# Sigmoid attention by pairs of heads: scores by halves of TensorE's rows, plain float32 sums for every head

## The chip, the core and the metric

One Trainium2 chip, of which one core is used. The metric is the device time of the program in microseconds. The kernel before takes 1150.06 us (median of three runs, 1149.88 to 1151.21). Its profile is of one execution of 1148.2 us.

The engines go by the profile's names: PE is TensorE's matrix products and PEld its weight loads, DVE is VectorE, ACT is ScalarE, POOL is GpSimd, SP is SyncE, which here only issues DMAs. Each engine works through its own queue in order.

## The reference

Three stages one after the other, for 4 batches of 448 tokens:

```python
scores = q @ k.transpose(0, 1, 3, 2) / sqrt(64) - log(448)   # 4 x 12 heads, 448 x 448
x = sigmoid(scores) @ v                                      # no softmax; heads side by side: 768 columns

h = maximum(x @ w_in, 0); u, v = h[..., :512], h[..., 512:]  # gated unit
v = normalised over its 512 columns
x = (u * (w_spatial @ v + b_spatial)) @ w_out

xn = normalised(x) * g_ln                                    # channel MLP, 768 -> 3072 -> 768
out = x + maximum(xn @ w_ch1, 0) @ w_ch2
```

The weights w_in, w_out, w_ch1 and w_ch2 come as numbers of 8 bytes.

## The kernel before, in words

**Products in parts.** A float32 number is split into a high part in the type float32r and a low part, the difference (`split`: a cast on ACT, a subtraction on DVE or POOL). A product of two such numbers is three products of parts (`mm3`, L246 to L248: high by high, high by low, low by high). A product of plain float32 is one instruction (it shows as two records in the trace) and needs no split, but goes over the data more often.

**Order.** Nothing is scheduled by the compiler: each engine's order is the order in which the Python code lays instructions out. Three mechanisms mix the work. The loop over heads lays out attention. A `Stream` named `bg` yields TensorE work of the gated unit (`hv`: x by the v half of w_in, 512 columns; `hu`: by the u half, 448 columns) in amounts counted in estimated us, `BG_0` and `BG_US` a head, and yields nothing as long as its inputs aren't there (`settled`: laid out `LAG` heads before). `Jobs` hands out pieces of the preparation of w_in and w_out: `load` (a DMA of 768 KB on SP's queue, into one of two raw buffers), `decode` (8 bytes to float32: L264 on ACT, L265, L266 and L269 on DVE) and `split` (L275 on ACT, L276 on DVE). w_in has 8 blocks of 768 columns, w_out 4. Heads from `FIRST` = 3 on hand out one piece each, from `MORE` = 14 on two; w_out's are queued after head `WO_FROM` = 38. After attention the rest of `bg` is laid out at once, then the last batch's `hv` and `hu`, `spatial`, the projection with w_out and the channel MLP.

**Scores** (`qk`, L433). A pair of heads is prepared together. Its tile `kk` holds k's high part in partitions 0 to 63 and k's low part in 64 to 127, and q's high part lies in both halves. For a chunk of 128 keys, one product over all 128 rows gives high by high plus low by high; a second over 64 rows, with k's high and q's low part, gives the third term. A head has four chunks, done in two calls of two: two 128-row products, two 64-row products, then one sigmoid (L438, ACT) over both chunks. High parts come by casting DMAs on POOL's queue (`qk_cast`, L367 and L368), the float32 numbers by SP's (`qk_load`, L377 and L378), and the low parts are subtracted by POOL (`qk_split`, L408 and L409; the first pairs by DVE). The first pair has its own path (`first_pair`).

**Weighted sums** (`av`). For heads 0 to 18 (`PLAIN`) four plain float32 products (L464) with v as weights, 64 columns wide, put in turn into the two column halves of the array, so that the two halves of the output's partitions hold parts of the sum. For the other 29 heads the sigmoids are split (`a_split`: L447 on ACT, L449, L451, L453, L454 on DVE), v is split (`v_split`), and seven products of parts over the full array follow (L470, L472); again each half of the partitions holds parts of the sum. In both cases `a_end` adds the halves (L484 copy on ACT, L485 add on DVE), and after two heads `x_split` splits x for the gated unit (by POOL from batch 2 on).

**Shapes.** TensorE's instructions thus come in three shapes: 128 rows by 128 columns (the high scores products, the split sums, all of the gated unit and MLP), 64 by 128 (the low scores products) and 128 by 64 (plain sums). PSUM has four banks for single tiles (`ps1`) and two tiles of two banks (`ps2`, scores).

Of the kernel before, what the change touches and what calls it, by code (L numbers as in the profile page):

```python
# [16 lines left out]
P = 128  # L17
# [21 lines left out]
# Matrix work of the gated unit beside each head, in us: in the first batch, and after.  # L39
BG_0, BG_US = 2.5, 2.2  # L40
# Heads after which what was laid out counts as there.
LAG = 2
WARM = 10
# The last batches whose low parts of v and x come from the vector engine.
V_POOL, X_POOL = 0, 1
# [10 lines left out]
R_ATT, F_ATT = 15872, 6208  # L56
R_MLP, F_MLP = 11904, 9984
# Where blocks lie after attention: none meets another while both are in use.
# [10 lines left out]
class Arena:  # L69
    """Columns of tiles that are given out and taken back while the program is laid out."""  # L70
# [89 lines left out]
class Jobs:  # L160
    """Pieces of work that are laid out between others, in order."""
# [42 lines left out]
def sigmoid_attention_gmlp_mlp(ctx: ExitStack, tc, q, k, v, w_in, w_sp, w_out, g_ln, w1, w2, out):  # L204
# [54 lines left out]
    def w_decode(raw):  # L259
# [3 lines left out]
        # The scale moves the exponent's offset from 1023 to 127; what float32 has not, goes to zero.  # L263
# [14 lines left out]
    class Chunk:  # L278
        """768 columns of a weight: load, decode and split are laid out apart."""
# [33 lines left out]
    def idle():  # L313
# [13 lines left out]
    # The blocks that stay past attention come first, from the base.  # L327
# [3 lines left out]
    x_r = Ring(F, S, 2)  # L331
    R.add("att", r_att)
    F.add("att", f_att)
    qh_r = Ring(R, 2 * S, 3, "att")
    ql_r = Ring(R, 2 * S, 2, "att")
    kk_r = Ring(R, 2 * SK, 3, "att")
    vv_r = Ring(R, 1024, 2, "att")
    ah_r = Ring(R, 4 * S, 2, "att")
    al_r = Ring(R, 3 * S, 2, "att")
    rv = Ring(F, 512, 3, "att")  # L340
    rq = Ring(F, 2 * S, 1, "att")
    rk = Ring(F, 2 * SK, 1, "att")
    af_r = Ring(F, 2 * S, 2, "att")
    tmp_r = Ring(F, S, 1, "att")
    v0_r = Ring(F, DH, 1, "att")
    a_rings = [v0_r, qh_r, ql_r, kk_r, vv_r, ah_r, al_r, rv, rq, rk, tmp_r]

    heads = [(b, h) for b in range(B) for h in range(H)]
    pairs = {}
    head = {}  # L350
# [6 lines left out]
    def plain(i):  # L357
        return i in PLAIN

    def on_pairs(f):  # L360
        return lambda p: f(p, *divmod(p, NPAIR)) if p < B * NPAIR else None

    @on_pairs
    def qk_cast(p, b, hp):
        """The high parts: q's in both halves of the partitions, k's in the first."""
        qh, kk = qh_r.next().ap(2, S), kk_r.next().ap(2, SK)
        nc.gpsimd.dma_start(kk[:D], k[b, hp])  # L367
        nc.gpsimd.dma_start(qh, q[b, hp])  # L368
        pairs[p] = dict(qh=qh, kk=kk)
# [10 lines left out]
    def first_pair():  # L380
        """The first pair's parts, head by head, without the wait for the casting DMAs."""
        qh, kk, ql = qh_r.next().ap(2, S), kk_r.next().ap(2, SK), ql_r.next().ap(2, S)
        qr, kr = rq.next().ap(2, S), rk.next().ap(2, SK)
        pairs[0] = dict(qh=qh, kk=kk, ql=ql)
        for j in range(2):
            nc.sync.dma_start(kr[:D, j], k[0, 0, :, j])
            nc.sync.dma_start(qr[:, j], q[0, 0, :, j])
        yield
        for j in range(2):
            nc.scalar.copy(kk[:D, j], kr[:D, j])  # L390
            nc.vector.tensor_copy(qh[:, j], qr[:, j])
            nc.vector.tensor_sub(kk[D:P, j], kr[:D, j], kk[:D, j])  # L392
            nc.vector.tensor_sub(ql[:D, j], qr[:D, j], qh[:D, j])
            yield
# [16 lines left out]
    @on_pairs  # L411
    def v_split(p, b, hp):
        t = pairs[p]
        vr = t["v"]
        vv = t["vv"] = vv_r.next().ap(8, 2, D)
        js = [j for j in range(2) if not plain(2 * p + j)]
        if js:
            cs = slice(4 * js[0], 4 * js[-1] + 4)
            split(vv[:, cs, 0, :], vv[:, cs, 1, :], vr[:, cs], nc.gpsimd if b > V_POOL else nc.vector)

    def qk(i, t):
        p, j = divmod(i, 2)
        a = pairs[p]
        if t == 0:
            head[i] = dict(af={})
            if not plain(i):
                head[i].update(ah=ah_r.next().ap(4, S), al=al_r.next().ap(3, S))
        ps = ps2()
        for part in ("qh", "ql"):
            rows = P if part == "qh" else D  # L430
            for cc in range(2):
                kc = slice((2 * t + cc) * P, (2 * t + cc + 1) * P)
                nc.tensor.matmul(  # L433
                    ps[:, cc, :S], a["kk"][:rows, j, kc], a[part][:rows, j],
                    start=(part == "qh"), stop=(part == "ql"),
                )
        af = af_r.next().ap(2, S)
        nc.scalar.activation(af, ps[:, :, :S], AF.Sigmoid, bias=bias_s, scale=1.0 / math.sqrt(D))  # L438
        head[i]["af"][t] = af

    def a_split(i, t, on_act):
        if plain(i):
            return
        h = head[i]
        ah, al, af = h["ah"], h["al"], h["af"].pop(t)
        if on_act:
            nc.scalar.copy(ah[:, 2 * t : 2 * t + 2], af)  # L447
        else:
            nc.vector.tensor_copy(ah[:, 2 * t : 2 * t + 2], af)  # L449
        if t == 0:  # L450
            nc.vector.tensor_sub(al[:, 0:2], af, ah[:, 0:2])  # L451
        else:
            nc.vector.tensor_sub(al[:, 2], af[:, 0], ah[:, 2])  # L453
            nc.vector.tensor_sub(ah[D:P, 3], af[D:P, 1], ah[D:P, 3])  # L454

    def av(i):
        p, j = divmod(i, 2)
        h = head[i]
        ps = ps1()
        for c in range(4):  # L460
            if plain(i):
                # In turn to the two halves of the array's columns, which run beside each other.
                rows = slice(D * (c % 2), D * (c % 2) + D)
                nc.tensor.matmul(  # L464
                    ps[rows, :S], pairs[p]["v"][:, 4 * j + c], h["af"][c // 2][:, c % 2],
                    start=(c < 2), stop=(c > 1),
                )
                continue
            w = pairs[p]["vv"][:, 4 * j + c].rearrange("p a d -> p (a d)")
# [5 lines left out]
    def a_end(i):  # L475
# [3 lines left out]
        if j == 0:  # L479
            pairs[p]["x"] = x_r.next().ap(S)  # L480
# [340 lines left out]
    for _ in pair0:  # L821
        pass
# [221 lines left out]
```

## Time and profile before

| | us |
|---|---|
| median of three runs | 1150.06 |
| profiled execution, first to last instruction | 1148.2 |
| busy: TensorE | 1131.0 |
| busy: VectorE | 727.0 |
| busy: ScalarE | 384.9 |
| busy: GpSimd | 218.2 |
| last scores product begins at | 293.3 |
| granted clock of TensorE, mean over the span | 0.991 of full speed |

A group's row in the profile has the line, engine, operation, what is written and read with shapes, the count, then the busy time in us, the mean length of one in ns, and the engine's idle time just before them with what ended it. A product's end in the trace is modelled, and products run into one another, so the distance between starts tells more than the length. Forms such as 64*128 are the rows and columns of the array that an instruction uses.

### The profile page before, as it was taken

What the parts mean: (1) busy time and instruction counts of PE and PEld (TensorE: products, weight loads), DVE (VectorE), ACT (ScalarE), POOL (GpSimd) and SP (SyncE); (2) the same over time, 40 slices, a digit from 0 to 9 for tenths busy, and PEclk for the clock granted to TensorE, in tenths of its full rate; (3) what the DMA queues carried; (4) which work ended last, traced back from release to release, by engine and by line L of the source; (5) the groups of instructions that cost most, each with busy time, mean ns of one, the idle gap of its engine ahead of it and who ended that gap; (6) DMA issues with size and microseconds to landing.
All of it is one profiled execution on the core that took longest, in us unless ns stands there. A gap on an engine that the chain in (4) does not pass through costs nothing.

```text
span 1148.2 us, 14874 instructions
## 1 busy us (share of the span) xinstructions
PE 1131.0 (99%) x6071; PEld 1019.7 (89%) x6071; DVE 727.0 (63%) x928; ACT 384.9 (34%) x586; POOL 218.2 (19%) x167
## 2 busy tenths in 40 slices
PE   8998999998999999999999999999999999999998
PEld 4445776776899999999999999999999999999998
DVE  3879999989677577545455555555554545555533
ACT  4776666665545243211112121111212112121100
POOL 2765556864221442000000000000000000000000
PEclk8999999998999999999999999999999999999999
DMA  9887444662641111111111111111111112020013
GB/s 251 234 220 196 119 129 122 151 186 86 216 133 65 69 56 56 55 56 55 56 56 56 55 56 55 55 56 56 56 56 55 56 36 76 28 83 28 28 74 120
DMA packets 33557, 104.81 MB, mean 91 GB/s; under 512 B 7568, under 2 KB 10128, under 8 KB 33360
## 3 DMA queue, kind: packets, MB, share of 16 engines
q1 hardware_dynamic: 26736, 79.93, 21.7%
q0 software_dynamic: 6752, 23.92, 8.0%
q8 instruction: 48, 0.79, 0.3%
q14 instruction: 21, 0.17, 0.1%
HBM read 90.98 MB, written 12.86 MB: 90 GB/s over the span
## 4 chain that ended last, share of the span: by engine, by line
PE 85%; DVE 9%; issue 3%; ACT 1%; DMA 0%; SPq 0%; ACTq 0%; DVEq 0%
PE ps L246 26%; PE ps L247 25%; PE ps L248 25%; PE ps L433 5%; DVE r_att L454 2%; DVE r_att L449 1%; PE ps L464 1%; PE ps L470 1%; DVE r_att L453 1%; DVE r_att L451 1%; DVE r_base L276 1%; DVE f_base L485 1%; DVE f_base L265 1%; PE ps L679 1%; PE ps L472 1%
## 5 line engine op out<-in xcount | busy, mean ns | idle before, releaser
L246 PE MATMUL ps<-r_base 128*128 128x384 f32 (+3 forms) x756 | 258.0, 341 | 0.0
L247 PE MATMUL ps<-r_base 128*128 128x384 f32 (+3 forms) x756 | 253.7, 336 | 0.1
L248 PE MATMUL ps<-r_base 128*128 128x384 f32 (+3 forms) x756 | 253.7, 336 | 0.0
L735 DVE TENSOR_TENSOR f_mlp<-ps,f_mlp 128x768 f32<-128x768 f32 (+1 forms) x157 | 149.5, 953 | 160.0 <-PE ps L248 159.9
L716 ACT ACTIVATE r_mlp<-ps 128x384 fp32r<-128x384 f32 (+1 forms) x120 | 56.4, 470 | 513.3 <-PE ps L248 513.3
L717 DVE SCALAR_TENSOR_TENSOR r_mlp<-ps,r_mlp 128x384 fp32r<-128x384 f32 (+1 forms) x120 | 63.5, 529 | 152.0 <-ACT r_mlp L716 152.0
L246 PEld LDWEIGHTS ps<-r_base 128*128 128x128 f32 x756 | 142.6, 189 | 16.7 <-issue 12.7
L248 PE MATMUL ps<-r_mlp 128*128 128x384 f32 (+1 forms) x460 | 154.5, 336 | 0.0
L246 PE MATMUL ps<-r_mlp 128*128 128x384 f32 x448 | 150.6, 336 | 0.0
L247 PE MATMUL ps<-r_mlp 128*128 128x384 f32 x448 | 150.3, 336 | 0.0
L248 PEld LDWEIGHTS ps<-r_base 128*128 128x128 f32 x756 | 142.8, 189 | 5.2
L247 PEld LDWEIGHTS ps<-r_base 128*128 128x128 f32 x756 | 142.8, 189 | 3.9 <-DVE r_base L276 0.4
L433 PE MATMUL ps<-r_att 64*128 64x448 f32 (+1 forms) x384 | 117.7, 408 | 3.6 <-DVE r_att L392 3.6
L433 PEld LDWEIGHTS ps<-r_att 64*128 64x128 f32 (+1 forms) x384 | 63.7, 192 | 54.3 <-issue 39.3
L246 PE MATMUL ps<-r_mlp,r_base 128*128 128x384 f32 (+1 forms) x304 | 105.3, 346 | 0.0
L247 PE MATMUL ps<-r_mlp,r_base 128*128 128x384 f32 (+1 forms) x304 | 104.3, 343 | 0.0
L248 PE MATMUL ps<-r_mlp,r_base 128*128 128x384 f32 (+1 forms) x292 | 99.8, 342 | 0.0
L438 ACT ACTIVATE f_att<-ps,bias_s 128x896 f32<-128x896 f32 x76 | 76.6, 1008 | 65.3 <-PE ps L433 30.2
L248 PEld LDWEIGHTS ps<-r_mlp 128*128 128x128 f32 x460 | 86.4, 188 | 0.2
L246 PEld LDWEIGHTS ps<-r_mlp 128*128 128x128 f32 x448 | 84.2, 188 | 0.0
L247 PEld LDWEIGHTS ps<-r_mlp 128*128 128x128 f32 x448 | 84.1, 188 | 0.0
L247 PE MATMUL ps<-r_base,r_mlp 128*128 128x384 f32 x224 | 76.3, 341 | 0.0
(120 smaller groups left out, 1681.5 us busy)
## 6 DMA issues: line engine op xcount, KB each, us to landing
f_base<-in_w SPq DMA_DIRECT2D x48, 768.0 KB, 4.2
r_att<-in_q POOLq DMA_DIRECT2D x23, 448.0 KB, 4.5
f_att<-in_v SPq DMA_DIRECT2D x24, 256.0 KB, 3.9
f_base<-in_w_in SPq DMA_DIRECT2D x8, 768.0 KB, 5.7
r_att<-in_k POOLq DMA_DIRECT2D x23, 256.0 KB, 4.0
f_att<-in_k SPq DMA_DIRECT2D x22, 256.0 KB, 3.5
f_att<-in_q SPq DMA_DIRECT2D x24, 224.0 KB, 3.5
out_y<-f_mlp SPq DMA_DIRECT2D x12, 384.0 KB, 2.3
```

The lines of the kernel that those rows point to most:

```text
L246: nc.tensor.matmul(ps, lh, rh, start=first, stop=False)
L247: nc.tensor.matmul(ps, lh, rl, start=False, stop=False)
L248: nc.tensor.matmul(ps, ll, rh, start=False, stop=last)
L265: nc.vector.tensor_scalar(bits, bits, 3, None, op0=ALU.logical_shift_left)
L276: eng.tensor_sub(lo, x, hi)
L433: nc.tensor.matmul(ps[:, cc, :S], a["kk"][:rows, j, kc], a[part][:rows, j], start=(part == "qh"), stop=(part == "ql"),)
L438: nc.scalar.activation(af, ps[:, :, :S], AF.Sigmoid, bias=bias_s, scale=1.0 / math.sqrt(D))
L449: nc.vector.tensor_copy(ah[:, 2 * t : 2 * t + 2], af)
L454: nc.vector.tensor_sub(ah[D:P, 3], af[D:P, 1], ah[D:P, 3])
L716: nc.scalar.activation(hh[:, f], ps[:, :n], AF.Relu)
L717: nc.vector.scalar_tensor_tensor(hl[:, f], ps[:, :n], 0.0, hh[:, f], op0=ALU.max, op1=ALU.subtract)
L735: nc.vector.tensor_add(y[:, hs], ps, y[:, hs])
```

## The change

Attention is done by pairs of heads instead of by heads, with one call for half a pair's keys. There are 48 such calls, as there were 48 heads.

- **Scores.** Head 0 of a pair has its q and k in partitions 0 to 63, head 1 in 64 to 127. All three terms are 64-row products, laid out in turn for the two heads, each head into its own bank of a `ps2` tile. A call does two chunks of both heads: twelve 64-row products. One sigmoid covers one chunk of both heads.
- **Preparation of q and k.** One load each of the float32 numbers on SP's queue, in pieces of 64 rows (the first pair's second head on ACT's queue); no casting DMAs. The high parts are cast by DVE (the first pair's k by ACT), the low parts are subtracted by POOL from the third pair on.
- **Weighted sums.** Plain float32 for all heads. Head 0 goes to column half 0, head 1 to column half 1, so that each half of the partitions holds one head's whole sum. `a_split`, `v_split` and `a_end` go, and x is split straight from PSUM by ACT and DVE (`x_end`).
- **Order.** A call lays out: scores, preparation of the next pair, the sums of the call before, the end of x, then 2.3 us of `bg` in one piece, then jobs. `bg` is asked from the first call on. Pieces of w_in come from call 1, two a call from call 4; w_out's from call 30.
- Buffers: six tiles of sigmoids, two each for high and low parts, two for raw q and k.

```diff
-BG_0, BG_US = 2.5, 2.2
+BG_US = 2.3
-FIRST, MORE = 3, 14
-WO_FROM = 38
+FIRST, MORE = 1, 4
+WO_FROM = 30
-PLAIN = range(19)
+PLAIN = range(B * H)
...
     @on_pairs
     def qk_load(p, b, hp):
-        t = pairs[p]
-        # The second pair's come while the first's are in use.
-        rings = (raw_r, raw_r) if p == 1 else (rq, rk)
-        t["raw"] = [r.next().ap(2, n) for r, n in zip(rings, (S, SK))]
-        nc.sync.dma_start(t["raw"][1][:D], k[b, hp])
-        nc.sync.dma_start(t["raw"][0][:D], q[b, hp, :D])
+        qr, kr = rq.next().ap(S), rk.next().ap(SK)
+        pairs[p] = dict(raw=(qr, kr))
+        for j in range(2):
+            rows = slice(D * j, D * j + D)
+            eng = nc.scalar if p == 0 and j else nc.sync
+            eng.dma_start(kr[rows], k[b, hp, :, j])
+            eng.dma_start(qr[rows], q[b, hp, :D, j])
...
     def qk_split(p, b, hp):
         t = pairs[p]
         qr, kr = t["raw"]
-        t["ql"] = ql_r.next().ap(2, S)
-        eng = nc.gpsimd if p > 2 else nc.vector
-        eng.tensor_sub(t["kk"][D:P], kr[:D], t["kk"][:D])
-        eng.tensor_sub(t["ql"][:D], qr[:D], t["qh"][:D])
+        (qh, ql), (kh, kl) = ([r.next().ap(n) for r in rs] for rs, n in ((q_r, S), (k_r, SK)))
+        t.update(qh=qh, ql=ql, kh=kh, kl=kl)
+        eng = nc.gpsimd if p > 1 else nc.vector
+        if p:
+            nc.vector.tensor_copy(kh, kr)
+        else:
+            nc.scalar.copy(kh, kr)
+        nc.vector.tensor_copy(qh, qr)
+        eng.tensor_sub(kl, kr, kh)
+        eng.tensor_sub(ql, qr, qh)
...
+    def qk(p, t):
+        a = pairs[p]
+        for c in (2 * t, 2 * t + 1):
+            ps = ps2()
+            kc = slice(c * P, (c + 1) * P)
+            for i, (w, x) in enumerate((("kh", "qh"), ("kl", "qh"), ("kh", "ql"))):
+                for j in range(2):
+                    rows = slice(D * j, D * j + D)
+                    nc.tensor.matmul(
+                        ps[:, j, :S], a[w][rows, kc], a[x][rows], start=(i == 0), stop=(i == 2)
+                    )
+            af = af_r.next().ap(2, S)
+            nc.scalar.activation(af, ps[:, :, :S], AF.Sigmoid, bias=bias_s, scale=1.0 / math.sqrt(D))
+            a["a", c] = af
+
+    def av(p, t):
+        a = pairs[p]
+        if t == 0:
+            a["ps"] = ps1()
+        for c in (2 * t, 2 * t + 1):
+            af = a.pop(("a", c))
+            for j in range(2):
+                rows = slice(D * j, D * j + D)
+                nc.tensor.matmul(
+                    a["ps"][rows, :S], a["v"][:, 4 * j + c], af[:, j], start=(c == 0), stop=(c == 3)
+                )
+
+    def x_end(p):
+        b, hp = divmod(p, NPAIR)
+        while b > 1 and len(gated) < b - 1:
+            bg.run(1.0)
+        xh, xl = (t[:, hp] for t in x_of(b))
+        split(xh, xl, pairs.pop(p)["ps"][:, :S])
+        x_done[b, hp] = now[0]
...
+    for i in range(2 * n_pairs):
+        p, t = divmod(i, 2)
         now[0] = i
+        qk(p, t)
+        if t == 0:
+            qk_split(p + 1)
+            qk_load(p + 2)
+        else:
+            pv_load(p + 2)
+        if i:
+            av(*divmod(i - 1, 2))
+            if t == 0:
+                x_end(p - 1)
+        bg.run(BG_US)
         jobs.pop(0 if i < FIRST else 2 if i >= MORE else 1)
```

Three places show what the change makes of the engines' orders. The changed kernel's lines are other ones: L392 are its scores, L408 its sums, L245 to L247 the three products of parts, L396 the sigmoids, L263 to L268 the decode, L274 and L275 the split, L375 and L378 the casts of k and q.

TensorE, before, in the second batch, from one head's scores over its sums to the next scores (ps is PSUM, r_att are attention's parts, r_base x and w_in):

```order
L433 MATMUL ps_733<-r_att 128x448 x4
L433 MATMUL ps_741<-r_att 128x448 x4
L470 MATMUL ps_752<-r_att 128x448
L472 MATMUL ps_752<-r_att 128x448
L470 MATMUL ps_752<-r_att 128x448
L472 MATMUL ps_752<-r_att 128x448
L470 MATMUL ps_752<-r_att 128x448
L472 MATMUL ps_752<-r_att 128x448
L470 MATMUL ps_752<-r_att 128x448
L433 MATMUL ps_763<-r_att 128x448 x4
L246 MATMUL ps_771<-r_base 128x448
L247 MATMUL ps_771<-r_base 128x448
```

And now, one call of the second batch:

```order
L392 MATMUL ps_623<-r_att 128x448 x6
L392 MATMUL ps_631<-r_att 128x448 x6
L408 MATMUL ps_640<-f_att 64x448 x4
L245 MATMUL ps_619<-r_base 128x512
L246 MATMUL ps_619<-r_base 128x512
L247 MATMUL ps_619<-r_base 128x512
```

Four products of two shapes have become twelve of one shape, the seven split sums four plain ones straight from the sigmoids (f_att), and the gated unit's products stand once in a call, behind the sums, instead of twice in a head.

VectorE, before, in the second batch, one head and the beginning of the next:

```order
L485 TENSOR_TENSOR f_base<-ps_1023,f_att 64x448
L449 CAST r_att<-f_att 128x896
L451 TENSOR_TENSOR r_att<-f_att,r_att 128x896
L453 TENSOR_TENSOR r_att<-f_att,r_att 128x448
L454 TENSOR_TENSOR r_att<-f_att,r_att 64x448
L485 TENSOR_TENSOR f_base<-ps_1070,f_att 64x448
```

And now, also in the second batch, one pair, that is two heads, with the statistics of a row block of the gated unit behind it (L473, L474, which stood between heads before):

```order
L375 CAST r_att<-f_att 128x512
L378 CAST r_att<-f_att 128x448
L275 TENSOR_TENSOR r_base<-ps_1108,r_base 128x448
L473 BN_STATS st_1160<-f_base 128x6
L474 BN_AGGR vraws<-st_1160 128x2
```

Five instructions a head have become three a pair.

ScalarE, before, in the first batch, three heads with the pieces of w_in between them (L264 decodes a block, L275 from f_base with 768 columns splits one):

```order
L438 ACTIVATE f_base<-ps_301,bias_s 128x896
L484 COPY f_att<-ps_293 64x448
L438 ACTIVATE f_base<-ps_309,bias_s 128x896
L275 CAST r_base<-f_base 128x448
L438 ACTIVATE f_att<-ps_329,bias_s 128x896
L484 COPY f_att<-ps_317 64x448
L438 ACTIVATE f_att<-ps_340,bias_s 128x896
L264 ACTIVATE f_base<-f_base 128x768
L438 ACTIVATE f_base<-ps_356,bias_s 128x896
L484 COPY f_att<-ps_346 64x448
L438 ACTIVATE f_base<-ps_364,bias_s 128x896
```

And now, also in the first batch, three calls:

```order
L396 ACTIVATE f_att<-ps_270,bias_s 128x896
L396 ACTIVATE f_att<-ps_278,bias_s 128x896
L263 ACTIVATE f_base<-f_base 128x768
L274 CAST r_base<-f_base 128x768
L396 ACTIVATE f_att<-ps_298,bias_s 128x896
L396 ACTIVATE f_att<-ps_306,bias_s 128x896
L274 CAST r_base<-ps_287 128x448
L263 ACTIVATE f_base<-f_base 128x768
L396 ACTIVATE f_att<-ps_336,bias_s 128x896
L396 ACTIVATE f_att<-ps_344,bias_s 128x896
L274 CAST r_base<-f_base 128x768
```

The sigmoids are as many; the copies of L484 are gone, and the decodes and splits of w_in, one in these rows before, are four.

More of the change, by code (lines that the diff above doesn't have):

```diff
@@ L38 @@
 WC = 768
-BG_0, BG_US = 2.5, 2.2
+BG_US = 2.3
 LAG = 2
 WARM = 10
-V_POOL, X_POOL = 0, 1
-FIRST, MORE = 3, 14
-WO_FROM = 38
+FIRST, MORE = 1, 4
+WO_FROM = 30
 VN_DVE = [range(4), range(4), (1, 3), (1, 3)]
 HU_EVERY = 3
-PLAIN = range(19)
+PLAIN = range(B * H)
 R_BASE, F_BASE = 23040, 7680
-R_ATT, F_ATT = 15872, 6208
+R_ATT, F_ATT = 3840, 8832
 R_MLP, F_MLP = 11904, 9984
@@ L313, in idle @@
     def idle():
+        pass
     now = [0]
@@ L330, in sigmoid_attention_gmlp_mlp @@
     xp = [R.alloc(KC * 2 * S), R.alloc(KC * 2 * S)]
-    x_r = Ring(F, S, 2)
     R.add("att", r_att)
     F.add("att", f_att)
[L334 to L339, printed above, removed]
-    rv = Ring(F, 512, 3, "att")
[L341 to L348, printed above, removed]
+    q_r = [Ring(R, S, 2, "att") for _ in range(2)]
+    k_r = [Ring(R, SK, 2, "att") for _ in range(2)]
+    rv = Ring(F, 512, 3, "att")
+    rq = Ring(F, S, 2, "att")
+    rk = Ring(F, SK, 2, "att")
+    af_r = Ring(F, 2 * S, 6, "att")
+    a_rings = [*q_r, *k_r, rv, rq, rk, af_r]
+    n_pairs = B * NPAIR
     pairs = {}
-    head = {}
     x_done = {}
@@ L355, in x_of @@
         return [t.ap(KC, 2, S)[:, :, b % 2] for t in xp]
-    def plain(i):
-        return i in PLAIN
     def on_pairs(f):
[L361 to L369, printed above, removed]
+        return lambda p: f(p, *divmod(p, NPAIR)) if p < n_pairs else None
     @on_pairs
     def qk_load(p, b, hp):
-        t = pairs[p]
-        rings = (raw_r, raw_r) if p == 1 else (rq, rk)
-        t["raw"] = [r.next().ap(2, n) for r, n in zip(rings, (S, SK))]
-        nc.sync.dma_start(t["raw"][1][:D], k[b, hp])
-        nc.sync.dma_start(t["raw"][0][:D], q[b, hp, :D])
[L380 to L384, printed above, removed]
-        for j in range(2):
[L386 to L394, printed above, removed]
+        qr, kr = rq.next().ap(S), rk.next().ap(SK)
+        pairs[p] = dict(raw=(qr, kr))
+        for j in range(2):
+            rows = slice(D * j, D * j + D)
+            eng = nc.scalar if p == 0 and j else nc.sync
+            eng.dma_start(kr[rows], k[b, hp, :, j])
+            eng.dma_start(qr[rows], q[b, hp, :D, j])
     @on_pairs
@@ L405, in qk_split @@
         qr, kr = t["raw"]
-        t["ql"] = ql_r.next().ap(2, S)
-        eng = nc.gpsimd if p > 2 else nc.vector
-        eng.tensor_sub(t["kk"][D:P], kr[:D], t["kk"][:D])
-        eng.tensor_sub(t["ql"][:D], qr[:D], t["qh"][:D])
[L411 to L419, printed above, removed]
@@ L421, in qk @@
-    def qk(i, t):
-        p, j = divmod(i, 2)
+        (qh, ql), (kh, kl) = ([r.next().ap(n) for r in rs] for rs, n in ((q_r, S), (k_r, SK)))
[22 more added lines that the diff above has]
+            a["a", c] = af
@@ L423, in qk @@
+    def av(p, t):
         a = pairs[p]
         if t == 0:
[L425 to L432, printed above, removed]
+            a["ps"] = ps1()
[3 more added lines that the diff above has]
+                rows = slice(D * j, D * j + D)
@@ L433, in qk @@
                 nc.tensor.matmul(
-                    ps[:, cc, :S], a["kk"][:rows, j, kc], a[part][:rows, j],
-                    start=(part == "qh"), stop=(part == "ql"),
-                )
[L437 to L469, printed above, removed]
-            nc.tensor.matmul(ps[:, :S], w, h["ah"][:, c], start=(c == 0), stop=(c == 3))
-            if c < 3:
-                nc.tensor.matmul(ps[:, :S], w, h["al"][:, c], start=False, stop=False)
-        h["ps"] = ps
@@ L475, in a_end @@
-    def a_end(i):
-        p, j = divmod(i, 2)
-        b, hp = divmod(p, NPAIR)
-        ps = head.pop(i)["ps"]
-        if j == 0:
-            pairs[p]["x"] = x_r.next().ap(S)
-        x = pairs[p]["x"][D * j : D * j + D]
-        tmp = tmp_r.next().ap(S)[D * j : D * j + D]
-        nc.scalar.copy(tmp, ps[D * (1 - j) : D * (2 - j), :S])
-        nc.vector.tensor_add(x, ps[D * j : D * j + D, :S], tmp)
-    def x_split(i):
-        p, j = divmod(i, 2)
-        b, hp = divmod(p, NPAIR)
-        if j == 1:
-            while b > 1 and len(gated) < b - 1:
-                bg.run(1.0)
-            xh, xl = (t[:, hp] for t in x_of(b))
-            split(xh, xl, pairs.pop(p)["x"], nc.gpsimd if b > X_POOL else nc.vector)
-            x_done[b, hp] = now[0]
+                    a["ps"][rows, :S], a["v"][:, 4 * j + c], af[:, j], start=(c == 0), stop=(c == 3)
+                )
@@ L564, in hu @@
         wh, wl = (t.ap(KC, DH) for t in wu)
-        while "u" not in vu or not all(settled(t.ready) for t in wu_chunks):
+        while not all(settled(t.ready) for t in wu_chunks):
             yield None
@@ L809, in sigmoid_attention_gmlp_mlp @@
     bg = Stream(gated_first(range(B - 1)))
-    vu = dict(v=v0_r)
-    more_af = [F.alloc(2 * S) for _ in range(2)]
-    af_r.blocks += more_af
-    pair0 = first_pair()
-    next(pair0)
-    qk_cast(1)
-    pv_load(0)
-    qk_load(1)
+    vu = dict(v=Ring(F, DH, 2), u=Ring(F, S, 2))
+    qk_load(0)
     for _ in range(WARM):
         nc.tensor.matmul(ps1()[:, :P], warm, warm, start=True, stop=True)
-    for _ in pair0:
-        pass
-    v_split(0)
+    qk_load(1)
+    pv_load(0)
+    qk_split(0)
     pv_load(1)
-    qk_split(1)
-    qk_cast(2)
-    qk_load(2)
-    pv_load(2)
     jobs.pop(2)
-    n_heads = len(heads)
-    for i in range(n_heads):
-        b = heads[i][0]
+    for i in range(2 * n_pairs):
+        p, t = divmod(i, 2)
         now[0] = i
-        if i == max(PLAIN) + 2:
-            af_r.blocks = [t for t in af_r.blocks if t not in more_af]
-            free_all(more_af)
-            vu.update(v=Ring(F, DH, 2), u=Ring(F, S, 2))
-        for t in range(2):
-            qk(i, t)
-            if t == 0 and i > 1:
-                a_end(i - 2)
-            if t == 1:
-                a_split(i, 0, False)
-                a_split(i, 1, True)
-                if i > 1:
-                    x_split(i - 2)
-                if i > 0:
-                    av(i - 1)
-            if i > 3:
-                bg.run(BG_US / 2 if i > H + 1 else BG_0 / 2)
-        p = i // 2
-        if i % 2 == 0:
-            v_split(p + 1)
-            if p:
-                pv_load(p + 2)
-        else:
-            qk_cast(p + 3)
-            qk_split(p + 2)
-            qk_load(p + 3)
+        qk(p, t)
+        if t == 0:
+            qk_split(p + 1)
+            qk_load(p + 2)
+        else:
+            pv_load(p + 2)
[4 more added lines that the diff above has]
+        bg.run(BG_US)
         jobs.pop(0 if i < FIRST else 2 if i >= MORE else 1)
@@ L864, in sigmoid_attention_gmlp_mlp @@
                 jobs.add([job, idle])
-    a_end(n_heads - 2)
-    bg.run(BG_US / 2)
-    av(n_heads - 1)
-    a_end(n_heads - 1)
-    x_split(n_heads - 1)
+    now[0] += 1
+    av(n_pairs - 1, 1)
+    bg.run(BG_US)
+    x_end(n_pairs - 1)
     now[0] = 10**9
@@ L872, in sigmoid_attention_gmlp_mlp @@
         r.free()
-    af_r.free()
     R.drop("att")
@@ L883, in sigmoid_attention_gmlp_mlp @@
     F.add("mlp", f_mlp)
-    x_r.free()
     wsp_b = R.at("mlp", 0, 8 * S)
```

## The prediction

> **What bounds the kernel now.** I read the page's busy shares first and then the table of stretches.
>
> ```profile
> span 1148.2 us, 14874 instructions
> PE 1131.0 (99%) x6071; PEld 1019.7 (89%) x6071; DVE 727.0 (63%) x928; ACT 384.9 (34%) x586; POOL 218.2 (19%) x167
> ```
>
> TensorE (PE) is busy for all but 17 us. The stretches say where those lie (columns: stretch, length, busy us of PE, weight loads, DVE, ACT, POOL, each with a count, then granted clock, DMA share, GB/s).
>
> ```profile
> 0.00:20.00 20.00, 15.32 (x47) 8.99 (x48) 8.23 (x14) 6.65 (x8) 3.64 (x10) 0.74 1.02 234
> 20.00:100.00 80.00, 79.92 (x319) 36.95 (x319) 62.87 (x53) 58.92 (x76) 50.24 (x34) 1.00 0.90 241
> 100.00:120.00 20.00, 16.96 (x64) 11.00 (x64) 19.06 (x24) 13.29 (x17) 10.36 (x8) 0.91 0.43 109
> 120.00:260.00 140.00, 137.83 (x568) 98.85 (x567) 132.91 (x122) 92.96 (x123) 92.14 (x61) 1.00 0.53 145
> 260.00:280.00 20.00, 16.25 (x58) 11.34 (x59) 19.54 (x19) 9.45 (x12) 9.82 (x5) 0.83 0.29 91
> ...
> 300.00:1144.00 844.00, 844.00 (x4931) 836.35 (x4930) 468.72 (x679) 189.94 (x333) 49.39 (x49) 1.00 0.19 65
> ```
>
> Attention is the first 300 us. From 300 on PE never pauses and the change does not touch that code, so the stretch moves as a block. Inside attention PE is full from 20 to 100. From 100 to 280 it idles 3.04 + 2.17 + 3.75 = 9.0 us, while DVE is busy 171.5 of 180 us; at the two worst places the clock also falls, which costs 0.09 x 17.0 + 0.17 x 16.3 = 4.3 us. So **TensorE is the bound, and VectorE takes about 13 us from it** between 100 and 280. Two questions decide: does TensorE get less to do, and is anything late that was not?
>
> **TensorE per head, before.** The timeline of TensorE (start, length, line) at a head with plain sums:
>
> ```profile
> 60.53 1.72 PE L464 MATMUL ps<-f_att 128*64 128x448 f32 x8
> 62.19 2.46 PE L433 MATMUL ps<-r_att 128*128 128x448 f32 x8
> 64.58 0.60 PE L464 MATMUL ps<-f_base,f_att 128*64 128x448 f32 x2
> ```
>
> Counted from start to start, the sums (L464, eight records for four products) take 1.66 us and the scores (L433) 2.39: **4.05 us a head**, switches of shape included. A head with split sums:
>
> ```profile
> 206.43 0.36 PE L247 MATMUL ps<-r_base 128*128 128x448 f32 x1
> 206.63 0.36 PE L248 MATMUL ps<-r_base 128*128 128x448 f32 x1
> 206.83 1.17 PE L433 MATMUL ps<-r_att 128*128 128x448 f32 x4
> 207.93 0.47 PE L470 MATMUL ps<-r_att 128*128 128x448 f32 x1
> 208.24 0.36 PE L472 MATMUL ps<-r_att 128*128 128x448 f32 x1
> 208.44 0.37 PE L470 MATMUL ps<-r_att 128*128 128x448 f32 x1
> ...
> 207.33 0.29 PEld L433 LDWEIGHTS ps<-r_att 64*128 64x128 f32 x2 [0.31 <-issue]
> ```
>
> A full-height product of 448 columns has a pitch of 0.20 to 0.205 us. The four scores products take 1.10 (206.83 to 207.93) instead of 0.82, and the next product 0.31 instead of 0.205. The weight load shows the two 64-row products starting at 207.33: full height runs 0.50 for two, 64 rows 0.60 for two, where 0.41 is the bare pitch. So a switch costs about 0.09 at its edge and 0.105 at the second product of the new shape. A half head's scores cost 1.10 + 0.105, and the seven split sums 7 x 0.205 = 1.43: 2 x 1.205 + 1.43 = **3.84 us a head**. With 19 plain and 29 split heads: 19 x 4.05 + 29 x 3.84 = **188.3 us**.
>
> **TensorE per call, after.** A call (48 of them, each the work of one head) has twelve 64-row score products, in turn to the upper and the lower half of the rows, then four plain sums. If halves run beside each other that is six pairs. No row of before has two row halves in turn, so the pitch of a pair is unknown. Its bounds: 0.19, from the column halves, and 0.41, two products one after the other.
>
> ```profile
> L464 PE MATMUL ps<-f_att x80: 539/539/1007, 16.6 to 103.2; 128*64 128x448 f32 x80
> ```
>
> Here eight records of 0.539 us go by in 1.66 us, 0.375 for each two: column halves do run beside each other. I take 0.205, a full-height product's pitch, since a pair streams as many columns; it is also nearest to the column halves. Scores: 6 x 0.205 = 1.23, and the switch 0.09 + 0.105 + 0.085 on the way out = 1.51. Sums: 1.66 as before (the moving data alternate between heads instead of between chunks, the form is the same). The first wide product after them: 0.105. Together 3.27 us; some ten calls have no wide product behind them and save 0.2. So 48 x 3.27 - 2 = **155 us, 33 less**. Making the 29 split heads plain is a loss inside that, 29 x (1.66 - 1.43) = 7 us; the scores pay for it. At a pitch of 0.19 it is 37 less; each 0.01 is 288 pairs x 0.01 = 2.9 us.
>
> A rule of the Trainium skill speaks against this: "TensorE: Matmul & The Clock Gate", Part 3, says that a weight load overlaps a running matmul only where the row groups differ. By it the third product of a run, whose weights go where the first still streams, would wait about the 0.105 us of a load, and a pair would take 0.31. The trace differs for full-height products, which use the same rows every time: after the switch at 207.93 the second waits 0.31, but the third follows 0.20 later. The same section measures 3.07 times for four row strips; at that efficiency a pair would take some 0.27 us (an estimate from that page), and the gain on TensorE would be about 15 us. No run here shows it.
>
> **VectorE, ScalarE, GpSimd.** What goes:
>
> ```profile
> L451 DVE TENSOR_TENSOR r_att<-f_att,r_att 128x896 fp32r<-128x896 f32 x28 | 48.5, 1732 | 1.0
> L453 DVE TENSOR_TENSOR r_att<-f_att,r_att 128x448 fp32r<-128x448 f32 x28 | 35.0, 1249 | 1.5 <-ACT r_att L447 1.5
> L454 DVE TENSOR_TENSOR r_att<-f_att,r_att 64x448 fp32r<-64x448 f32 x28 | 32.8, 1171 | 0.9
> L485 DVE TENSOR_TENSOR f_base<-ps,f_att 64x448 f32<-64x448 f32 x48 | 29.9, 622 | 15.7 <-ACT f_att L484 14.1 <-issue 0.3
> L449 DVE CAST r_att<-f_att 128x896 fp32r<-128x896 f32 x28 | 27.7, 991 | 0.4
> L391 DVE CAST r_att<-f_att 128x448 fp32r<-128x448 f32 x2 | 0.8, 394 | 8.4 <-DMA f_att<-in_q 8.4
> ```
>
> That is 174 us off VectorE. What comes, for each of 24 pairs, is two casts (0.39 by the last row, and at most 0.99 by the cast of 896 columns; I take 0.45 for 512) and a subtraction out of PSUM (0.62, as L485): 1.5 us, 36 in all, beside a pair's 6.5 us or more of TensorE. VectorE then has slack everywhere after the first batch, and of the 13 us I take **10 back**; 0 and 13 are the ends. GpSimd's differences have 128 rows by 512 and 448 columns in place of 64 rows by 1024 and 896; they start two calls ahead of their use and are hidden by that.
>
> **What is late next: the first batch.** The pieces of w_in's preparation now come two a call from the fourth call, where before it was one a head until the fourteenth. Per call that is two thirds of a block.
>
> ```profile
> L438 ACT ACTIVATE f_att<-ps,bias_s 128x896 f32<-128x896 f32 x76 | 76.6, 1008 | 65.3 <-PE ps L433 30.2 <-DVE r_att L451 19.6 <-DVE r_att L454 12.4
> L264 ACT ACTIVATE f_base<-f_base 128x768 f32<-128x768 f32 x60 | 53.9, 899 | 4.0 <-DVE r_base L276 3.0 <-DMA f_base<-in_w_in 0.8
> L275 ACT CAST r_base<-f_base 128x768 fp32r<-128x768 f32 x40 | 33.3, 831 | 32.3 <-DVE f_base L269 19.5 <-PE ps L248 12.8
> L275 ACT CAST r_base<-f_base 128x448 fp32r<-128x448 f32 x24 | 13.5, 561 | 8.1 <-DVE f_base L485 8.0
> L276 DVE TENSOR_TENSOR r_base<-f_base,r_base 128x768 fp32r<-128x768 f32 x40 | 43.2, 1080 | 6.2 <-ACT r_base L275 6.2
> L266 DVE SCALAR_TENSOR_TENSOR f_base<-f_base 128x768 uint32<-128x768 uint32 x60 | 59.3, 988 | 2.1
> L265 DVE TENSOR_SCALAR f_base<-f_base 128x768 uint32<-128x768 uint32 x60 | 43.1, 718 | 2.3 <-ACT f_base L264 2.2
> f_base<-in_w_in SPq DMA_DIRECT2D x8, 768.0 KB, 5.7
> ```
>
> ScalarE per call: 2 x 1.008 + half an x cast (0.28, by the cast of 448 columns) + 2/3 x (0.899 + 0.831) = 3.45 us. VectorE: 0.75 + 2/3 x (0.718 + 2 x 0.988 + 1.080) = 3.27. TensorE without wide products: 3.08. For some nine calls ScalarE, not TensorE, sets the pace: 9 x 0.37 = 3.3 us. Behind it stands a chain: two raw buffers, so a block's load waits for the decode two blocks earlier (about 3.6 us on ScalarE and VectorE) and lands 5.7 us later, 9.3 in the 10 us that three calls take; on SyncE's queue the loads of q and k, now issued there in 64-row pieces, stand behind such a load, and a decode that waits holds the sigmoids behind it on ScalarE. It fits, narrowly; with landings of twice 5.7 a round takes 15 us, and four rounds (eight blocks) cost 4 x 5 = 20 us. I take **4 lost**, ends 0 and 20. What keeps me near the low end is attention's own traffic, in the stretch where DMA stood at 0.90 to 1.02:
>
> ```profile
> r_att<-in_q POOLq DMA_DIRECT2D x23, 448.0 KB, 4.5
> f_att<-in_v SPq DMA_DIRECT2D x24, 256.0 KB, 3.9
> r_att<-in_k POOLq DMA_DIRECT2D x23, 256.0 KB, 4.0
> f_att<-in_k SPq DMA_DIRECT2D x22, 256.0 KB, 3.5
> f_att<-in_q SPq DMA_DIRECT2D x24, 224.0 KB, 3.5
> ```
>
> A pair's 1440 KB become 736, since GpSimd's two casting loads go.
>
> At the start, the chain that ended last has the first two heads' scores so:
>
> ```profile
> 7.17 3.41 PE ps L433 x8
> ...
> 12.45 4.21 PE ps L433 x8
> ```
>
> TensorE stands 1.9 us between them for the second head. Now both heads of the first pair arrive together: I take **2 gained**, ends 0 and 4.
>
> **Sum.** From the profiled execution: 1148.2 - 33 - 10 + 4 - 2 = 1107. The median of the runs shown is 1.9 us above this execution's span: **1109 us**.
>
> **The rivals.**
> 1. Row halves take turns (a pitch of 0.41). Place: the scores of all 48 calls; price 288 x 0.205 = 59 us against the 33 + 8 gained, so 1168, slower. It decides from a pitch of about 0.35. For it: no row shows two row halves at once. Against: column halves do it, in all 80 records of the group above.
> 2. The weights of a half wait for the product running in it (0.31): 288 x 0.105 = 30 us given back, 1139.
> 3. Pairs overlap but not fully (0.24 to 0.29): 1119 to 1133.
> 4. The first batch's chain binds at its upper end, the rest as forecast: 1109 + 16 = 1125.
> 5. The change does little: VectorE's 174 us were never the bound, so without a gain on the scores 10 us would be all that is left of it, less the 7 of the plain sums. This is the case between 1 and 2, near 1150.
>
> **How the numbers follow.** Forecast (pitch 0.19 to 0.23) 0.66, partly overlapping 0.09, waiting weights 0.07, first batch 0.04, turns 0.12, no change 0.02. Faster by over 0.2%, which is about what a measurement of this kernel tells from no change (2.3 us): 0.85; within it 0.02; slower 0.13. The range runs from 1097 (pitch 0.19, every stall gone) to 1139, through rival 2; what it leaves out is turns and no change.
>
> **What would show it.** Right: in the changed kernel's timeline a run of twelve score products goes by in about 1.5 us, the group's summed lengths well above its busy time; VectorE at half load or less after 100 us; no stretch below 19.5 of 20 us busy on TensorE after the first batch; the last scores near 260 us, where now they are at 293. Wrong: twelve products in 2.1 us (waiting weights) or 2.7 (turns); sigmoids that wait for decodes, and TensorE for them, between 20 and 55 us; or idle time on TensorE after attention, where now there is none.

## The result, and the profile after

| | before | after |
|---|---|---|
| median | 1150.49 us (4 runs, 1149.88 to 1151.21) | 1100.58 us (4 runs, 1098.17 to 1102.86) |
| profiled execution, span | 1148.2 us | 1101.1 us |
| busy: VectorE | 727.0 us | 547.6 us |
| busy: ScalarE | 384.9 us | 320.8 us |
| busy: GpSimd | 218.2 us | 104.8 us |

The ratio is 0.956, with a 95% interval from 0.955 to 0.958: the change is faster by 4.4%. The prediction was 1109 us, within 1097 to 1139.

The stretches of the changed kernel, with the columns as before (length, busy us of PE, weight loads, DVE, ACT, POOL, each with a count, then granted clock, DMA share, GB/s):

```profile
0.00:20.00 20.00, 16.27 (x92) 9.68 (x92) 6.45 (x15) 11.64 (x14) 0.20 (x4) 1.00 0.82 209
20.00:40.00 20.00, 17.94 (x89) 8.83 (x89) 14.69 (x20) 12.46 (x15) 7.99 (x6) 0.83 0.71 214
40.00:60.00 20.00, 19.65 (x123) 9.88 (x124) 15.86 (x24) 16.84 (x21) 6.68 (x5) 1.00 0.79 232
60.00:80.00 20.00, 20.00 (x106) 12.05 (x103) 9.48 (x15) 10.79 (x14) 6.71 (x6) 1.00 0.30 90
...
120.00:260.00 140.00, 140.00 (x766) 87.35 (x765) 26.57 (x53) 62.77 (x78) 28.54 (x27) 1.00 0.37 108
260.00:280.00 20.00, 20.00 (x94) 17.32 (x93) 16.66 (x28) 11.27 (x16) 3.02 (x3) 1.00 0.74 240
```

From 60 us to 1094 us TensorE is busy all the time and the clock is full; VectorE, which had 133 us of 140 to do between 120 and 260, has 27. What is left are 6.1 us of idle TensorE in the first 60 us, a slow clock between 20 and 40, and 3.6 us of idle time in the last 7 us (3.5 before).

One call in TensorE's timeline (start, length, line):

```profile
130.03 1.48 PE L392 MATMUL ps<-r_att 64*128 64x448 f32 x12
131.44 1.72 PE L408 MATMUL ps<-f_att 128*64 128x448 f32 x8
133.10 0.50 PE L245 MATMUL ps<-r_base 128*128 128x512 f32 x1
```

From start to start the twelve 64-row products take 1.41 us. That is six steps of about 0.2 us with the cost of the switch: the two halves run beside each other. The groups say the same (busy time, then mean length in ns):

```profile
L392 PE MATMUL ps<-r_att 64*128 64x448 f32 x576 | 74.6, 387 | 5.1 <-DVE r_att L378 2.4 <-POOL r_att L380 1.3 <-ACT f_att L396 0.7
L275 DVE TENSOR_TENSOR r_base<-ps,r_base 128x448 fp32r<-128x448 f32 x24 | 15.0, 623 | 103.7 <-ACT r_base L274 103.7
L375 DVE CAST r_att<-f_att 128x512 fp32r<-128x512 f32 x23 | 9.8, 425 | 27.5 <-PE ps L392 17.3 <-DMA f_att<-in_k 10.2
L378 DVE CAST r_att<-f_att 128x448 fp32r<-128x448 f32 x24 | 9.3, 387 | 4.4 <-DMA f_att<-in_q 4.3
```

576 products of 0.387 us are 223 us of products in 74.6 busy us, 3.0 times as much. That is not three at a time, as a product's modelled length runs past its pitch: where the halves take turns (experiment 1) the same quotient is 220 / 134.6 = 1.6. The three rows of VectorE are all that it has left of attention's steady work: 34.1 us where 174 stood.

### The profile page after: what moved, and what is told of

It is laid out like the page before. It is cut to its first block, busy times and chain, and to the rows that moved or that the text cites. A ratio compares the mean times of both kernels' runs of the same rounds, so it can differ in the third digit from the quotient of the medians.

```text
span 1101.1 us, 15020 instructions
## 1 busy us (share of the span) xinstructions
PE 1091.3 (99%) x6292; PEld 983.8 (89%) x6292; DVE 547.6 (50%) x817; ACT 320.8 (29%) x493; POOL 104.8 (10%) x96
## 4 chain that ended last, share of the span: by engine, by line
PE 95%; DMA 2%; DVE 1%; issue 1%; POOL 0%; ACT 0%; SPq 0%; POOLq 0%; DVEq 0%; ACTq 0%
PE ps L245 28%; PE ps L246 28%; PE ps L247 27%; PE ps L408 6%; PE ps L392 5%; DMA f_att<-in_k 1%; PE ps L602 1%; DMA f_att<-in_q 0%; POOL r_att L380 0%; PE ps L542 0%; PE ps L541 0%; DVE f_base L265 0%; DVE f_base L264 0%; ACT f_att L396 0%; DVE r_base L275 0%
## 5 line engine op out<-in xcount | busy, mean ns | idle before, releaser
L245 PE MATMUL ps<-r_base 128*128 128x384 f32 (+3 forms) x756 | 257.6, 341 | 0.0
L247 PE MATMUL ps<-r_base 128*128 128x384 f32 (+3 forms) x756 | 253.2, 335 | 0.0
L245 PEld LDWEIGHTS ps<-r_base 128*128 128x128 f32 x756 | 142.3, 188 | 31.4 <-issue 25.4
L247 PE MATMUL ps<-r_mlp 128*128 128x384 f32 (+1 forms) x460 | 154.6, 336 | 0.0
L245 PE MATMUL ps<-r_mlp 128*128 128x384 f32 x448 | 150.5, 336 | 0.0
L247 PEld LDWEIGHTS ps<-r_base 128*128 128x128 f32 x756 | 142.5, 188 | 5.1
L396 ACT ACTIVATE f_att<-ps,bias_s 128x896 f32<-128x896 f32 x96 | 91.6, 1005 | 76.4 <-PE ps L392 76.1
L245 PE MATMUL ps<-r_mlp,r_base 128*128 128x384 f32 (+1 forms) x304 | 105.4, 347 | 0.0
L247 PE MATMUL ps<-r_mlp,r_base 128*128 128x384 f32 (+1 forms) x292 | 99.8, 342 | 0.0
L247 PEld LDWEIGHTS ps<-r_mlp 128*128 128x128 f32 x460 | 86.4, 188 | 0.2
L408 PE MATMUL ps<-f_att 128*64 128x448 f32 x384 | 84.3, 560 | 0.0
L245 PEld LDWEIGHTS ps<-r_mlp 128*128 128x128 f32 x448 | 84.2, 188 | 0.0
L392 PE MATMUL ps<-r_att 64*128 64x448 f32 x576 | 74.6, 387 | 5.1 <-DVE r_att L378 2.4
L392 PEld LDWEIGHTS ps<-r_att 64*128 64x128 f32 x576 | 50.9, 188 | 30.3 <-issue 16.6
```

What stands on the lines that cost most here:

```text
L245: nc.tensor.matmul(ps, lh, rh, start=first, stop=False)
L247: nc.tensor.matmul(ps, ll, rh, start=False, stop=last)
L392: nc.tensor.matmul(ps[:, j, :S], a[w][rows, kc], a[x][rows], start=(i == 0), stop=(i == 2))
L408: nc.tensor.matmul(a["ps"][rows, :S], a["v"][:, 4 * j + c], af[:, j], start=(c == 0), stop=(c == 3))
```

## The experiments

The kernel before, run beside them, took 1150.2 to 1150.7 us (medians). Where no interval is given, it is one run.

**1. Both heads on the same rows.** The scores of each pair's second head are left out here: the products take the first head's q and k.

```diff
                 for j in range(2):
-                    rows = slice(D * j, D * j + D)
+                    rows = slice(0, D)
```

> The changed kernel with both heads' score products in the upper half of the rows (partitions 0 to 63), so that no product has the other half of the array beside it; the second head of each pair gets the first head's scores. Theory (the row halves run beside each other, a pair of products has a pitch of 0.203 us instead of two times that): a run of twelve takes 2.65 us from start to the sums' start instead of 1.43, 48 x 1.22 = 58 us more, so about 1159 us, slower than the kernel before. Rival A (the saving came from fewer switches of shape, and the halves share nothing): a run stays at 1.43 and the time at 1101. Rival B (a run is held by its weight loads, not by the products): a run of about 1.9 us, near 1123.

Measured: 1158.8 us. One call of this kernel in TensorE's timeline:

```profile
140.99 2.70 PE L392 MATMUL ps<-r_att 64*128 64x448 f32 x12
143.62 1.73 PE L408 MATMUL ps<-f_att 128*64 128x448 f32 x8
```

The run takes 2.63 us from start to the sums' start, against 1.41. Nothing else was changed, so running side by side is worth 48 x 1.22 = 58.6 us (the times differ by 58.2), and without it the whole change would be 8.6 us slower than the kernel before beside it. Rivals A and B fall.

**2. The same twelve products, three of a head in a row.**

```diff
-            for i, (w, x) in enumerate((("kh", "qh"), ("kl", "qh"), ("kh", "ql"))):
-                for j in range(2):
+            for j in range(2):
+                for i, (w, x) in enumerate((("kh", "qh"), ("kl", "qh"), ("kh", "ql"))):
```

> The changed kernel with the same twelve products, in another order: three of the first head, then three of the second, for each chunk. Theory (two products run side by side only when the next in the queue is for the other half, since they start in order): of six products only the third and fourth, and the last and the next chunk's first, can start together, so nine steps instead of six: a run of 2.04 us, 48 x 0.61 = 29 us more, about 1130. Rival (the engine looks ahead and starts a product of the free half early): a run of 1.43 and 1101.

Measured: 1101.8 us, and in the timeline:

```profile
128.69 1.49 PE L392 MATMUL ps<-r_att 64*128 64x448 f32 x12
130.12 1.72 PE L408 MATMUL ps<-f_att 128*64 128x448 f32 x8
```

1.43 us, as with products in turn. I had expected that a product starts only after those ahead of it in the queue have started; that was wrong. The trace has the second head's first product 10 ns behind the first head's first, though two others stand between them in the queue. (A record does not name its half; that the two products that start together belong to the two heads follows from experiment 1, where products of one half never start together.) So for TensorE's products the sentence at the beginning, that each engine works through its own queue in order, does not hold across the two row halves.

**3. Six in a row,** to see how far that goes.

```diff
-        for c in (2 * t, 2 * t + 1):
-            ps = ps2()
+        two = {c: ps2() for c in (2 * t, 2 * t + 1)}
+        for j in range(2):
+            rows = slice(D * j, D * j + D)
+            for c, ps in two.items():
...
```

> The changed kernel with six products of the first head in a row (both chunks), then six of the second. In the run with three in a row each product of the free half started about 10 ns after the other half's, which the in-order theory excluded. New theory J (each row half has its own line of waiting products, fed in order much faster than they run): a run of twelve stays at 1.43 us with the second head's products some 20 ns behind, 1100. Rival K (the look ahead reaches only a few instructions): the second head's products start late, a run of 1.6 us or more, 48 x 0.2 = 10 us or more, 1110 or above.

Measured: 1122.4 us. The timeline (the sums are L409 here):

```profile
131.69 1.99 PE L392 MATMUL ps<-r_att 64*128 64x448 f32 x12
133.61 1.72 PE L409 MATMUL ps<-f_att 128*64 128x448 f32 x8
```

1.92 us, 0.5 more a call, 48 x 0.5 = 24 us. The records start at 131.69, 132.00, 132.20 for the first head and at 132.20 for the second: the second half began when the third of the six began and three were waiting. So it is rival K's side, with a reach of about three waiting products as far as these two runs show, enough for three in a row and not for six.

**4. Plain sums alone,** in the kernel before.

```diff
-PLAIN = range(19)
+PLAIN = range(B * H)
```

with the buffers of the splits taken out and four tiles of sigmoids throughout.

> The kernel before with plain float32 sums for all 48 heads, and its scores as they were: one part of the change alone. It takes the splits of the sigmoids and of v from VectorE, ScalarE and GpSimd. Theory (TensorE pays 0.21 us a head for plain sums, 29 heads, 6 us; the stalls between 100 and 280 us, 9 us of idle time and 4 of slow clock, go): 1150 + 6 - 13 = 1143. Rival C (VectorE's relief is what made the change fast, and the scores little): 1115 or less. Rival D (VectorE was hidden all along): 1156.

Measured: 1140.45 us, ratio 0.991 (0.988 to 0.994). Its stretches:

```profile
100.00:120.00 20.00, 20.00 (x86) 10.66 (x84) 10.62 (x14) 13.15 (x18) 11.98 (x8) 1.00 0.57 143
120.00:260.00 140.00, 140.00 (x588) 81.91 (x587) 22.33 (x39) 67.46 (x89) 66.12 (x49) 1.00 0.52 145
260.00:280.00 20.00, 20.00 (x88) 11.87 (x86) 9.18 (x8) 9.24 (x12) 6.79 (x4) 1.00 0.34 104
```

TensorE idles no longer between 100 and 280, and the clock no longer falls. The theory's sign and place hold, and rivals C and D fall. With the 6 us that plain sums add, the stalls were worth 9.7 + 6 = about 16 us, more than the 13 that I read from busy time and clock. In the kernel before, TensorE's waits between 100 and 280 us are for VectorE alone (who waits, for whom, us in total, times, longest):

```profile
PE ps L470 <- DVE r_att L449: 2.4, 1, 2.4
PE ps L470 <- DVE r_att L454: 2.4, 5, 1.7
PE ps L472 <- DVE r_att L453: 2.4, 3, 1.6
PE ps L472 <- DVE r_att L451: 1.7, 3, 0.6
```

The experiment takes more away than these lines, though: ScalarE has 34 us and GpSimd 31.5 us less to do, and there are four tiles of sigmoids where the kernel before has two from head 20 on. Whether more tiles with the splits kept would have brought part of the 16 was not tried.

**5. Four kernels beside each other on one chip.** First the changed kernel again:

> The changed kernel once more, beside the next three on the same chip: 1100 us, as on record (1098.2 to 1102.9).

Measured: 1099.65 us (1098.22 to 1101.01), ratio 0.955 (0.953 to 0.958).

Loads of q and k three pairs ahead:

```diff
-    rq = Ring(F, S, 2, "att")
-    rk = Ring(F, SK, 2, "att")
+    rq = Ring(F, S, 3, "att")
+    rk = Ring(F, SK, 3, "att")
...
     pv_load(0)
+    qk_load(2)
     qk_split(0)
...
-            qk_load(p + 2)
+            qk_load(p + 3)
```

> The changed kernel with q and k loaded three pairs ahead instead of two (three raw buffers), the third pair's ahead of the first two blocks of w_in on the queue. Theory (what TensorE still loses in the first 60 us, 6.1 us idle and some 3 of slow clock, is mostly the third pair waiting behind w_in's blocks: a load of k that lands 10.5 us late): the stop near 20 us goes, 4 to 6 us less, about 1095. Rival E (ScalarE and VectorE set the pace there through the decodes): no change, 1100.

Measured: 1097.83 us (1097.27 to 1099.78), ratio 0.954 (0.951 to 0.957). The chain that ended last says what was meant, in the changed kernel's profile first:

```profile
9.01 10.54 DMA f_att<-in_k
...
21.51 1.45 POOL r_att L380
23.00 1.86 PE ps L392 x8
```

The third pair's k, issued behind two blocks of w_in, takes 10.5 us, and GpSimd's differences and TensorE follow it. With the loads ahead the stretch from 20 to 40 us has

```profile
20.00:40.00 20.00, 19.82 (x123) 10.38 (x125) 15.10 (x23) 16.31 (x21) 8.34 (x7) 1.00 0.98 258
```

so 0.2 us idle and a full clock, against 0.9 idle and 0.91 in the execution of the changed kernel beside it (2.1 and 0.83 in the one shown above). So the wait at this place goes. In sum TensorE idles no less: 4.15 us in the first 60 us against 3.97 beside it, since the first 20 us have 0.9 more. What is left is the slow clock, 0.09 x 19.06 = 1.7 us. In the time it is 1.8 us, less than forecast, and the intervals overlap.

The gated unit's products in every second call:

```diff
-        bg.run(BG_US)
+        if t:
+            bg.run(2 * BG_US)
```

> The changed kernel with the gated unit's products in every second call, twice as many: scores, sums, scores, sums, wide. Theory (a switch of shape costs 0.09 us at its edge and 0.105 at the second product): a pair has five switches instead of six, 22 pairs x 0.2 = 4 us less, about 1096. Rival F (without wide products between, the sigmoids of a call are not done when the next but one wants their PSUM): a wait on ScalarE in every second call gives it back, 1100 or more.

Measured: 1097.37 us (1096.02 to 1099.02), ratio 0.953 (0.951 to 0.956), 2.3 us under the changed kernel beside it. The list of waits of this kernel has

```profile
PEld ps L392 <- ACT f_att L396: 18.9, 27, 1.3
```

where the changed kernel has 7.1 us, 11 times: rival F's wait is there too, 12 us more of it on the weight loads. But the records show no price for it: in all 17 calls after 60 us in which scores follow sums directly, they start 0.475 to 0.476 us behind the start of the last two records of the sums, as a wide product does in the changed kernel (0.476). The wait lies under running products, and rival F falls. The gain is smaller than the 4 us that five switches instead of six were to bring, and the intervals overlap, so its size is not shown.

w_in as late as before:

```diff
-FIRST, MORE = 1, 4
+FIRST, MORE = 3, 14
```

> The changed kernel with the pieces of w_in as late as before (one a call from call 3, two from call 14). Theory (the dense pieces cost the first batch some 3 us in waits and nothing later): 0 to 4 us less, 1097 to 1100, since the work that TensorE does is the same and what it misses early it does later. Rival G (with w_in late, the wide products run out and attention has nothing to fill the waits with): slower by 3 us or more.

Measured: 1107.31 us (1106.23 to 1108.9), ratio 0.962 (0.959 to 0.965): slower by 8 us. Its stretches, and the wait of TensorE and the ScalarE row that belong to it:

```profile
20.00:40.00 20.00, 18.96 (x101) 8.83 (x101) 12.22 (x17) 12.12 (x14) 9.70 (x8) 0.83 0.61 188
40.00:60.00 20.00, 20.00 (x127) 10.54 (x127) 10.67 (x17) 15.30 (x19) 7.48 (x7) 1.00 0.62 187
...
280.00:300.00 20.00, 15.73 (x63) 13.43 (x62) 13.23 (x24) 9.50 (x18) 4.57 (x6) 0.85 0.44 124
```

```profile
PE ps L245 <- ACT f_base L498: 3.9, 1, 3.9
```

```profile
294.12 0.54 ACT L498 ACTIVATE f_base<-ps 128x448 f32<-128x448 f32 x1 [5.09 <-DMA uscr<-f_base]
```

The theory falls on both counts. Early, the slow place from 20 to 40 stays with thin pieces, so they weren't its cause; only 0.35 us of idle time between 40 and 60 go. (The loads of the first two blocks are laid out before the first call and are as early here as in the changed kernel.) Late, TensorE stands 4.3 us after attention, and the clock of 0.85 there costs 0.15 x 15.73 = 2.4 more: the relu of a u block waits for a buffer whose store is late on SyncE's queue, and TensorE waits for the relu to free its PSUM tile. Rival G has the sign and not the place. That this wait comes from the shifted order is read from the trace and wasn't tried by itself.

**6. Split sums again, with the row halves kept** (from the second batch on).

```diff
-PLAIN = range(B * H)
+PLAIN = range(12)
...
+            if t == 0:
+                nc.vector.tensor_copy(ah, af)
+            else:
+                nc.scalar.copy(ah, af)
+            if c < 3:
+                nc.vector.tensor_sub(al, af, ah)
+            else:
+                nc.vector.tensor_sub(ah[D:P], af[D:P], ah[D:P])
...
+            if t == 0:
+                a["ps"] = [ps1(), ps1()]
```

> The changed kernel with split sums again from the second batch on (36 heads): sigmoids and v are split, seven full-array products a head, the halves added. One part of the change undone, with the row halves kept. Theory (plain sums cost TensorE 0.21 us a head and buy the relief of VectorE): TensorE gets 36 x 0.21 = 7.6 us less; VectorE goes from a fifth to about four fifths busy between 100 and 250 us and GpSimd has the splits of v and x again, so stalls of 0 to 10 us come back: 1092 to 1103. Rival H (VectorE's stalls come wherever sums wait for splits): 1105 or more, with TensorE waiting for the splits' lines. Rival I (with the scores shorter, VectorE keeps up): 1092, a version that is better.

Measured: 1134.37 us (1131.57 to 1135.24), ratio 0.985 (0.982 to 0.988): 34 us slower than the changed kernel. TensorE's busy share and the waits of its products (PE) and weight loads (PEld):

```profile
120.00:260.00 140.00, 125.30 (x655) 95.85 (x655) 98.72 (x131) 89.83 (x127) 60.53 (x45) 0.98 0.36 102
```

```profile
PE ps L432 <- DVE f_att L459: 17.6, 13, 3.6
...
PEld ps L432 <- DVE f_att L459: 10.4, 17, 2.8
...
PEld ps L434 <- DVE r_att L411: 4.9, 5, 1.6
...
PEld ps L432 <- DVE r_att L413: 3.4, 8, 0.6
...
PE ps L434 <- DVE r_att L411: 3.2, 5, 1.4
```

Rival H has the size, but its cause only in part. VectorE is 70% busy. TensorE is idle 35.7 us in this execution, against 9.8 in the changed kernel's. Its products wait 17.6 us for L459, the addition of the two halves that frees a PSUM tile (a pair now holds two of the four), and 3.2 us for the split L411. The waits of the weight loads lie in part in the same idle time and in part under running products, so they can't be added to these. So this shows what split sums cost in this layout; with PSUM laid out otherwise they weren't tried.

**7. Both edits with the lower medians,** loads ahead and wide products in every second call.

> The changed kernel with both edits that were faster alone: q and k loaded three pairs ahead, and the gated unit's products in every second call. Theory (different places, 0 to 60 us and 60 to 250 us, so they add): 1100 - 2 - 2 = 1096 or a little less. Rival: no better than either alone, 1097 to 1098.

Measured: 1096.62 us (1095.89 to 1097.5), ratio 0.952 (0.949 to 0.955). It has the lowest median of all. Against the changed kernel's 1099.65 and 1100.58, neither run beside it, it is 3.0 and 4.0 us; the differences are as small as the spread of the runs, so whether the gains of 1.8 and 2.3 add can't be told.

## Why the prediction was right, point by point

**TensorE's work, 33 us less: right.** It rested on one number that no row of before showed, the pitch of two products in two row halves. I took 0.205 us, a full-height product's; the run of twelve took 1.41 us where the terms give 1.42. The sums took 1.66, as carried over. The first experiment shows that the pitch is the cause and its price: 58.6 us of the forecast's 59, and with the halves in turn the change would have been slower (1158.8; the rival had 1168, as it kept less of the other gains). The waiting weights (0.31) and the partial overlap (0.24 to 0.29, and the 0.27 estimated from the Trainium skill's page "TensorE: Matmul & The Clock Gate") did not occur.

**VectorE's stalls, 10 us back: the term that was sized wrongly.** Plain sums alone gave 9.7 us net of the 6 that they add, so 16. In the step "I take 10 back; 0 and 13 are the ends" the upper end was too low: idle time in the table of stretches misses short gaps, because a product's modelled length (0.36 us for a pitch of 0.2) covers the start of a gap. In the records of the kernel before between 100 and 280 us, starts lie in sum some 15 us further apart than is usual at the same place in the order, slow clock included, 13 of it at the split sums (L470, L472), where the idle time is 9.0. Experiment 4 relieved ScalarE and GpSimd too and gave more tiles, so that all 16 are VectorE's is argued, not shown.

**The first batch, 4 lost and 2 gained: about right in size, in part wrong in cause.** The first 100 us have 6.15 us of idle TensorE where before had 4.75; the other profiled execution of the changed kernel (experiment 5) has 3.97, so the size differs between executions by more than the 2 us forecast net. The forecast's chain had loads of q and k standing behind blocks of w_in, and that is what TensorE waited for at 20 us: one load of k behind two blocks (10.5 us instead of the median 3.4). But it came to TensorE over VectorE's casts and GpSimd's differences, which the forecast called hidden, and not over decodes that hold the sigmoids back. The way over the decodes and the raw buffers shows in the chain only later and costs 0.35 us, at 55 us. Late pieces of w_in left the place at 20 us as it was; with an earlier load of q and k the wait between 20 and 40 went.

**The sum.** 33 + 16 - 1.4 = 47.6 us against the 47.1 between the two spans. The 33 in it is the forecast itself. A check without it is the step from plain sums alone (experiment 4, 1140.45) to the changed kernel (1100.58 and 1099.65): 40 to 41 us, with the new order and loads in it, where the forecast has 33 + 6 = 39. Of the 8 us by which the prediction was too high, 6 are the term of the stalls; the rest is that the median lies 1.9 us above the profiled span before, and 0.5 below it after.

**The signs.** The run of twelve (1.41 us), TensorE without a pause after the first batch and the last scores (251 us, forecast near 260) came as named. VectorE is busy 19% of the time between 120 and 260 us, but 16.66 of 20 us between 260 and 280, where attention is over.

## What to carry to other kernels

When the rows of a kernel leave one price open, work out the two ends that it can have and what each makes of the sum: here 0.205 or 0.41 us a pair decided between 4% faster and 1% slower. A full engine hides another's load until it waits for it in order: in experiment 4 VectorE's 143 us less (727.0 to 583.7 busy), with what ScalarE and GpSimd had less, brought about 16, and the products laid side by side brought 59. On a DMA queue, look at which transfers are issued ahead of the first one that is needed, not only at the total traffic.

## What the runs showed of the hardware

- Two 64-row float32r products of 448 columns in the two halves of the rows start 1 to 4 ns apart in the call shown, and the pairs have the pitch of one full-height product, 0.203 us. With both on one half (experiment 1) each takes 0.203.
- Products for the two row halves do not start strictly in the order of the queue: with three in a row for one half the run took 1.43 us, with six in a row 1.92, so that in these two runs the other half's products passed two and three waiting ones, and not four or five. The Trainium skill, "TensorE: Matmul & The Clock Gate", Part 3, has products start in the queue's order; the second experiment differs, and the measurement decides.
- A change between shapes of the array cost 0.08 to 0.1 us at its edge and 0.105 us at the second product, before and after alike; where plain sums with 64 columns of weights follow, 0.05 at the second.
